# A fused attention and two-stage mixing kernel on one core: v of head 0, the staging of w_theta, the branch flag and the queue of loads are rearranged

## Chip, core and metric

The kernel runs on one core of one Trainium2 chip. The metric is the device time of one execution in microseconds (us); lower is better. The time before is the median of three runs, and one further execution was profiled.

## What is computed

Three layers follow each other, all in float32, for a batch of 2, 8 heads, 768 positions and 64 columns per head (so 16 heads in all and a model width of 512):

```python
# attention: a key counts if it is one of the first n_global or among the last n_local positions
scores = q @ k.T / sqrt(64) + bias                       # bias: -slope(head) * distance
a = softmax(where(keep, scores, -1e9)); x = a @ v        # heads side by side: x is 768 x 512
# mixing layer
theta = x @ w_theta
y = w_tok_r @ (x * cos(theta)) + w_tok_i @ (x * sin(theta))
u = x + y;  x2 = u + relu(u @ w_ch)
# feed-forward layer with a gate
h = relu(x2 @ w_in);  out = (h * sigmoid(conv3(h))) @ w_out
```

n_global is 8 and n_local is 96 here. The weights arrive as float64 bit patterns and are turned into float32 on the chip.

## The kernel before, in words

**Head of the program.** `begin` (line 1031) loads the two integers, q and k of heads 0 and 1, and builds the bias table. The integers decide by a flag (`fi`, line 1072) which of two programs runs: the fast one when both are small enough, a general one otherwise. Every engine loads the flag into a register (line 1022) and branches (line 1025). On VectorE that load stands behind the five instructions that finish the bias table (lines 1076 to 1080). Behind the branch, `run_fast` (line 860) makes ScalarE and GpSimd clear halves of staging tiles (lines 865, 866), lets GpSimd scale the bias table for head 1 (`tables`, line 336), and starts SyncE's queue with v of head 0 (`load_v`, line 274), q and k of heads 2 and 3 (`pair`) and v of head 1.

**Attention as a pipeline of steps.** The loop at line 903 counts steps j. Step j = 3i + tp treats head i, two blocks of 128 queries at a time. In step j TensorE makes the scores of step j; VectorE the bias, minimum and copy of step j-1 (`softmax`, line 372); ScalarE the exponentials of j-2 (line 381); TensorE the transposes of j-3 (line 390); ScalarE copies those of j-4 out (line 84); TensorE multiplies with v for j-5; and VectorE divides a finished head by its row sums (`normalise`, lines 290 to 292). Each engine works through its own list in the order in which the Python program emits it, and waits on semaphores only. So a "step" orders the list of an engine; it does not hold a queue back until TensorE gets there.

**Two ways of preparing q and k.** Heads 0 to 7 (`WHOLE`) are used as float32 straight from the load. Heads 8 to 15 are split into a rounded high part and a low part. For head i+1 this is done during head i: ScalarE makes the high part of q (line 300, at tp 0), VectorE its low part (line 304, at tp 1), and VectorE the low part of k (line 92, at tp 2). The high part of k is not computed: GpSimd's queue loads k a second time with a cast (`keys`, line 256, "the casting load", 408 KB), at tp 2, into the buffer that the head before the last one has just finished with. The low part of k needs this casting load and a plain load of k.

**SyncE's queue.** For heads 8 to 15 the plain loads are q (384 KB) at tp 2 of head i-3, k's second copy (204 KB) at tp 0 of head i-2 (both line 251), and v (357.5 KB) at tp 0 of the head itself. SyncE issues them strictly in the order of its list, each as soon as the buffer's last reader is done.

**The weight conveyor.** `Net.weight` queues a job per weight block, `Net.fetch` (line 121) puts its load on SyncE's queue when its staging tile is free, and `Net.conveyor` spends a few instructions on it per step: one on ScalarE (line 100), three on VectorE (lines 104, 108, 112), then the rounding (line 84) and the rest (line 92). Through the attention stage there are two staging tiles, `wst0` and `wst1`, which the jobs use in turn: jobs 0 to 3 are w_theta, jobs 4 to 11 the first half of w_tok. The next job but one is fetched when the third VectorE instruction of a job has freed its tile. The conveyor rests while heads 8 to 10 run (line 967).

Of the kernel before, what the change touches and what calls it, by code (L numbers as in the profile page):

```python
# [12 lines left out]
F32 = mybir.dt.float32  # L13
F32R = mybir.dt.float32r
I32 = mybir.dt.int32
# [4 lines left out]
B, H, S, D = 2, 8, 768, 64  # L20
DM, DFF = H * D, 1024
P = 128
# [3 lines left out]
NH = B * H  # L26
# [6 lines left out]
NV = 2 * NT - 1  # L33
VW = D + 1
HALF = S // 2
SLOT = 3072
STAGE = S + NT * KW
# [5 lines left out]
WHOLE = range(8)  # L43
# [9 lines left out]
class Net:  # L53
# [67 lines left out]
    def fetch(self):  # L121

        while self.loaded < self.limit:
            j = self.jobs[self.loaded]
            tag, x = j["where"]
            w = 2 * j["width"]
            if tag not in self.open or any(t == tag and x < b and a < x + w for t, a, b in self.held.values()):
                return
            self.held[self.loaded] = (tag, x, x + w)
            if tag == "scratch":  # L130
                j["st"] = self.head["scratch"][:, x : x + w].bitcast(I32)
            else:
                j["st"] = self.small.tile([P, 1024], I32, tag=tag, name=self.uid(tag))[:, :w]
            self.nc.sync.dma_start(j["st"], j["src"].bitcast(I32))
            self.loaded += 1
# [91 lines left out]
class Attention:  # L227
# [48 lines left out]
    def V(self, i):  # L276
        return self.v[i % 3].rearrange("p (t c) -> p t c", t=NV)
# [29 lines left out]
class FastAttention(Attention):  # L307
# [3 lines left out]
    def __init__(self, net, xs):  # L311
# [4 lines left out]
        self.whole = [x[:, 0:S], x[:, STAGE : STAGE + S], y[:, STAGE : STAGE + S], y[:, 0:S]]  # L316
        self.both = [x[:, S:STAGE], y[:, S:STAGE]]

    def half(self, i):
        return slice(D * (i % 2), D * (i % 2) + D)  # L320

# [138 lines left out]
class Mix:  # L460
# [6 lines left out]
    def begin(self):  # L467
        n = self.net
        self.xT = [n.slot(f"xT{b}", [P, KC, S], F32, "xT") for b in range(2)]
        wth = n.slot("w", [P, 2, KC, DM], F32R, "wth")  # L470
        self.wth = [wth[:, i] for i in range(2)]
        self.r = n.slot("r", [P, NT, DM], F32, "r")
        src = n.io["w_theta"].rearrange("(c p) n -> c p n", p=P)
        for c in range(KC):
            n.weight(src[c], DM, lambda c=c: (self.wth[0][:, c], self.wth[1][:, c]), (f"wst{c % 2}", 0))
        self.wt = [[n.slot("p0", [P, 4, 2, HALF], F32R, "wt"), n.slot("p1", [P, 4, 2, HALF], F32R, "wt"), None], [None] * 3]
        self.wch, self.win, self.wout = [None] * KC, [None] * NF, [None] * NF
        ring = [("wst0", 0), ("wst1", 0), ("scratch", 0), ("scratch", 2 * HALF), ("scratch", 4 * HALF)]
        for x in range(2 * NT * 2):
            hf, k = divmod(x, 2 * NT)  # L480
            s, ri = divmod(k, 2)

            def tok(hf=hf, k=k):
                w = self.wt[hf][k // 4]
                return None if w is None else (w[:, k % 4, 0], w[:, k % 4, 1])

            n.weight(n.io["w_tok"][NT * ri + s, :, HALF * hf : HALF * hf + HALF], HALF, tok, ring[k % 5] if hf else ring[k % 2])

        def of(ws, i):
            return lambda: None if ws[i] is None else (ws[i][:, 0], ws[i][:, 1])  # L490

        ring = [("wst0", 0), ("wst1", 0), ("scratch", 0)]
        src = n.io["w_ch"].rearrange("(c p) n -> c p n", p=P)
        late = [(src[c], self.wch, c) for c in range(KC)]
        late += [(n.io["w_in"][f], self.win, f) for f in (6, 7, 0, 1, 2, 3, 4, 5)]
        src = n.io["w_out"].rearrange("(f p) n -> f p n", p=P)
        late += [(src[f], self.wout, f) for f in range(NF)]
        for x, (src, ws, i) in enumerate(late):
            n.weight(src, DM, of(ws, i), ring[x % 3] if x < KC + NF else ring[x % 2])
        n.open = {"wst0", "wst1"}  # L500
        n.limit = 12

    def alloc_xTs(self):
# [194 lines left out]
    def tail(self, early):  # L698
# [20 lines left out]
            self.theta_part(t, th[t], (3,))  # L719
        ring.extend((("O", 2), ("O", 2), ("X", 1), ("PT", 2)))  # L720
        banks = [bank() for _ in range(KC)]
        turns = n.small.tile([P, 1024], I32, tag="wst0", name=n.uid("turns")).bitcast(F32)
        red = [self.reduce_theta(th[t], r[t], turns[:, DM * t : DM * t + DM]) for t in range(2)]
        for chain in (red[0], red[1], early, red[0]):
            next(chain, None)
# [134 lines left out]
def run_fast(tc, net):  # L860
# [2 lines left out]
    att = FastAttention(net, xs)  # L863
    mix = Mix(net, xs)
    nc.scalar.activation(att.whole[3][0:D], net.head["half_pi"][0:D].to_broadcast([D, S]), AF.Copy, scale=0.0)
    nc.gpsimd.memset(att.whole[2][D:P], 0.0)
    att.tables(1)
    att.load_v(0)
    att.pair(2)
    att.load_v(1)  # L870
    mix.begin()
# [31 lines left out]
    for j in range(NJ + LAG_N + 3):  # L903
# [14 lines left out]
        if 0 <= j - LAG_PV < NJ:  # L918
            att.pv(j - LAG_PV)
        jj = j - LAG_N  # L920
        for h in range(NH):
            if jj == 3 * h + 2 + (h in LATER):
                att.normalise(h, att.o.pop(h))
# [5 lines left out]
        if i > 0 and i + 1 not in WHOLE:  # L929
            if tp == 0:  # L930
                att.split(i + 1, "  A")
            else:
                att.split(i + 1, ("   V", " V")[tp - 1])
        if tp == 1 and i > 0 and i + 2 in WHOLE and i % 2 == 0:
            att.pair(i + 2)
        if tp == 2 and i + 3 < NH and i + 3 not in WHOLE:
            att.load(i + 3, slice(0, S))
        if tp == 0 and i + 2 < NH and i + 2 not in WHOLE:
            att.load(i + 2, slice(S, STAGE), slice(D, P))
        if i > 0 and tp == 2 and i + 1 in WHOLE:  # L940
            att.load_v(i + 1)
        if tp == 0 and i < NH and i not in WHOLE:
            att.load_v(i)
        last.step()
        jj = j - LAG_N - 1
# [18 lines left out]
            next(early, None)  # L964
        if j == 4:
            net.fetch()
        if 6 < j < NJ and i not in (8, 9, 10):
            net.run((3, 2, 3)[tp] if i > 10 else 2)
    last.drain()
# [3 lines left out]
def run_general(tc, net):  # L973
# [5 lines left out]
    for i in range(NH):  # L979
# [5 lines left out]
            att.unit(i, t, o)  # L985
        att.normalise(i, o)
    mix.begin()
    net.finish(12)
    for b in range(2):
        mix.alloc_xTs()  # L990
# [25 lines left out]
def build(nc, io):  # L1016
    with tile.TileContext(nc) as tc, tc.tile_pool(name="const", bufs=1) as small:
        head = {}
        net = Net(tc, io, small, None, None, head)
        with tc.tile_pool(name="idle", bufs=1, space=bass.MemoryType.PSUM) as ps, tc.manual_schedule():  # L1020
            begin(nc, io, net, small, head, ps.tile([P, 512], F32, name="idle"))
        rv = nc.values_load(
            head["flag"][:1, :1], min_val=0, max_val=1, skip_runtime_bounds_check_because="it is the product of comparisons, 0 or 1"
        )
        with tc.If(rv == 1) as cmp:
            arm(tc, io, head, run_fast)
        with cmp.Else():
            arm(tc, io, head, run_general)
# [2 lines left out]
def begin(nc, io, net, small, head, idle):  # L1031
# [4 lines left out]
    for x in range(0, NT, 2):  # L1036
        k, q = slice(x * KW, x * KW + 2 * KW), slice(x * P, x * P + 2 * P)
        nc.scalar.dma_start(scratch[:, S:STAGE][:, k], io["pairs"][0, :, k])
        nc.sync.dma_start(scratch[0:D, q], io["qk"][0, 0:D, 0, q])
    nc.sync.dma_start(scratch[D:P, STAGE : STAGE + S], io["qk"][0, D:P, 1, 0:S])  # L1040
    nc.vector.memset(scratch[D:P, 0:S], 0.0)
    zero = nc.const_aps.tensor(0.0, [P, 512], F32)
    for x in (512, 512, 256):
# [29 lines left out]
    far = small.tile([P, NG], F32, name="far")  # L1073
    nc.gpsimd.tensor_scalar(far, R[:, G], ng, BIG, op0=ALU.is_ge, op1=ALU.mult)
    nc.gpsimd.tensor_scalar(far, far, nl, FIRST, op0=ALU.max, op1=ALU.mult)
    nc.vector.tensor_scalar(T, R, 1.0 / FIRST, nl, op0=ALU.mult, op1=ALU.is_ge)  # L1076
    nc.vector.scalar_tensor_tensor(T, T, FIRST * BIG, R, op0=ALU.mult, op1=ALU.min)  # L1077
    nc.vector.tensor_copy(X, T[:, O])
    nc.vector.tensor_tensor(X[:, 0:NG], X[:, 0:NG], far, op=ALU.max)
    nc.vector.tensor_copy(T[:, G], far)  # L1080
    nnl = small.tile([P, 1], F32, name="nnl")
    head.update(scratch=scratch, qk0=qk0, table=table, ident=ident, half_pi=hp[:, 0:1], ng=ng, nl=nl, nnl=nnl, flag=fi)


# [34 lines left out]
```

## Time and profile before

| | us |
|---|---|
| median of three runs | 405.25 (404.54, 405.25, 405.83) |
| the profiled execution, its own time | 404.36 |
| span of that execution, first to last instruction | 402.6 |

The span is cut into instructions per engine. TensorE appears twice: PE is its matmuls, PEld its weight loads. DVE is VectorE, ACT ScalarE, POOL GpSimd, SP SyncE. A group's row gives how often it ran, its busy time and mean duration, and how long the engine idled before it and on whom it waited. The chain of waits is followed from the last instruction backwards, at each step to whatever released it. The timeline gives start and duration of each instruction or run of like instructions. DMA rows say how long a load took from issue to landing.

### The profile page before, as it was taken

To read this page: it belongs to the slowest core of one execution; us is meant where nothing else is said; L and a number is where in the kernel's file an instruction comes from. 1 tells how busy PE (TensorE), PEld (TensorE's weight loads), DVE (VectorE), ACT (ScalarE), POOL (GpSimd) and SP (SyncE) were. 2 spreads that over 40 slices of the span, in tenths; PEclk is the share of its full clock that TensorE was granted. 3 is DMA by queue.
4 is the path that set the end of the run, shared out by engine and by line. 5 is a ranking of instruction groups with operands and counts; after the bars stand their busy time and mean duration, and the time that the engine had idled before them with its cause. 6 is when DMAs were issued, how large, how long until landed. Compare 5 with 4: busy or idle time off the path is not lost.

```text
span 402.6 us, 6479 instructions
## 1 busy us (share of the span) xinstructions
PE 396.0 (98%) x2382; PEld 374.4 (93%) x2382; DVE 321.8 (80%) x708; ACT 224.7 (56%) x439; POOL 26.0 (6%) x36
## 2 busy tenths in 40 slices
PE   8999999999999999999999999999999999999995
PEld 5999999999988999999999999999999998888885
DVE  6788999998878869999899999998999999700001
ACT  5888888787887787235355346555654554300000
POOL 5214123121000000000000000000000000000000
PEclk9999999999999999999999999999999999999998
DMA  7978798855000330246464433130000000210111
GB/s 191 314 230 247 216 268 232 246 153 157 0 2 0 117 89 33 78 145 172 155 206 163 157 104 106 53 105 2 0 2 0 2 0 2 78 52 34 45 52 60
DMA packets 16023, 42.94 MB, mean 107 GB/s; under 512 B 2160, under 2 KB 2992, under 8 KB 15984
## 3 DMA queue, kind: packets, MB, share of 16 engines
q1 hardware_dynamic: 13968, 38.44, 30.8%
q0 software_dynamic: 1152, 3.34, 3.0%
q10 hardware_dynamic: 864, 0.68, 0.6%
q8 instruction: 20, 0.33, 0.3%
q14 instruction: 19, 0.16, 0.1%
HBM read 39.31 MB, written 3.15 MB: 105 GB/s over the span
## 4 chain that ended last, share of the span: by engine, by line
PE 96%; DMA 2%; DVE 1%; issue 0%; DVEq 0%
PE O L95 26%; PE S L95 23%; PE PT L95 17%; PE TH L95 15%; PE X L95 9%; PE PT L390 4%; DMA qk<-qk 1%; PE X L514 1%; DMA words<-n 1%; DVE qk L92 0%; DVE scratch L88 0%; DVE table L1077 0%; PE TH L514 0%; PE O L514 0%; DVE table L1076 0%
## 5 line engine op out<-in xcount | busy, mean ns | idle before, releaser
L381 ACT ACTIVATE a<-a,nm 128x232 f32<-128x232 f32 (+1 forms) x96 | 39.8, 466 | 4.7 <-DVE nm L372 4.6
L95 PE MATMUL O<-a,a 128*128 128x65 f32 x236 | 29.9, 268 | 0.0
L100 ACT ACTIVATE wbit<-wst 128x512 f32<-128x512 f32 (+1 forms) x38 | 23.2, 614 | 11.2 <-DMA wst<-w_ch 4.7
L95 PEld LDWEIGHTS O<-a,a 128*128 128x128 f32 x236 | 29.0, 192 | 0.2
L84 ACT ACTIVATE a<-PT 128x512 f32<-128x512 f32 (+1 forms) x48 | 26.5, 552 | 3.8 <-PE PT L390 3.6
L372 DVE CUSTOM_DVE_ANT_0 a<-S,qk 128x232 f32<-128x232 f32 (+1 forms) x72 | 24.0, 371 | 5.0 <-PE PT L390 4.9
L390 PE MATMUL PT<-ident,a 128*128 128x128 f32 x176 | 27.1, 273 | 0.0
L95 PE MATMUL O<-wt,z 128*128 128x384 f32 x144 | 26.9, 334 | 0.0
L95 PE MATMUL TH<-wth,xTs 128*128 128x512 f32 x96 | 26.2, 408 | 0.0
L104 DVE TENSOR_SCALAR wbit<-wbit 128x512 int32<-128x512 int32 (+1 forms) x48 | 18.9, 395 | 8.7 <-ACT wbit L100 8.7
L95 PE MATMUL PT<-wt,z 128*128 128x384 f32 x132 | 25.8, 334 | 0.0
L84 ACT ACTIVATE wt<-wbit 128x384 fp32r<-128x384 f32 x24 | 12.5, 520 | 23.3 <-DVE wbit L112 13.7
L95 PEld LDWEIGHTS O<-wt,z 128*128 128x128 f32 x144 | 25.2, 188 | 0.1
L112 DVE SCALAR_TENSOR_TENSOR wbit<-wst,wbit 128x512 int32<-128x512 int32 (+1 forms) x38 | 23.8, 627 | 1.1
L108 DVE SCALAR_TENSOR_TENSOR wbit<-wst,wbit 128x512 int32<-128x512 int32 (+1 forms) x38 | 23.8, 626 | 1.0
L95 PEld LDWEIGHTS PT<-wt,z 128*128 128x128 f32 x132 | 23.1, 188 | 0.0
L390 PEld LDWEIGHTS PT<-ident,a 128*128 128x128 f32 x176 | 20.8, 141 | 1.3
L95 PE MATMUL S<-wt,z 128*128 128x384 f32 x120 | 22.0, 335 | 0.0
L336 POOL TENSOR_SCALAR qk<-table 128x360 fp32r<-128x360 f32 x15 | 18.3, 1222 | 41.2 <-DVE nm L372 28.8
L95 PEld LDWEIGHTS S<-wt,z 128*128 128x128 f32 x120 | 20.9, 188 | 0.0
L95 PEld LDWEIGHTS TH<-wth,xTs 128*128 128x128 f32 x96 | 17.0, 189 | 3.1
L95 PE MATMUL O<-x,win 128*128 128x384 f32 x96 | 17.4, 336 | 0.0
(216 smaller groups left out, 940.6 us busy)
## 6 DMA issues: line engine op xcount, KB each, us to landing
wst<-w_tok SPq DMA_DIRECT2D x18, 384.0 KB, 3.5
a<-v SPq DMA_DIRECT2D x16, 357.5 KB, 5.2
wst<-w_out SPq DMA_DIRECT2D x8, 512.0 KB, 3.2
qk<-qk POOLq DMA_DIRECT2D x8, 408.0 KB, 5.4
a<-qk SPq DMA_DIRECT2D x8, 384.0 KB, 5.0
out<-scratch SPq DMA_DIRECT2D x11, 256.0 KB, 2.0
wst<-w_in SPq DMA_DIRECT2D x5, 512.0 KB, 4.3
scratch<-w_tok SPq DMA_DIRECT2D x6, 384.0 KB, 3.4
```

The lines of the kernel that those rows point to most:

```text
L84: self.nc.scalar.activation(out, in_, AF.Copy)
L95: self.nc.tensor.matmul(out, l, r, start=start, stop=stop)
L100: self.nc.scalar.activation(t.bitcast(F32), w[:, 1 : w.shape[1] : 2].bitcast(F32), AF.Copy, scale=REBIAS)
L104: self.nc.vector.tensor_scalar(t, t, 3, None, op0=ALU.logical_shift_left)
L108: self.nc.vector.scalar_tensor_tensor(t, w[:, 0 : w.shape[1] : 2], 29, t, op0=ALU.logical_shift_right, op1=ALU.bitwise_or)
L112: self.nc.vector.scalar_tensor_tensor(t, w[:, 1 : w.shape[1] : 2], -(1 << 31), t, op0=ALU.bitwise_and, op1=ALU.bitwise_or)
L336: self.nc.gpsimd.tensor_scalar(self.bias[i % 2], self.net.head["table"], x / FIRST, None, op0=ALU.mult)
L372: self.nc.vector.tensor_tensor_reduce(self.sS[tp][:, c], s["sp"][:, c], t, scale=QSCALE if i in WHOLE else 1.0, scalar=3.0e38, op0=ALU.add ...
L381: self.nc.scalar.activation(sS[:, c], sS[:, c], AF.Exp, bias=s["nm"][:, u : u + 1], scale=-1.0)
L390: self.nc.tensor.transpose(pt[:, c], sS[:, self.columns(u, a)], net.head["ident"])
L514: self.nc.tensor.transpose(xb[:, P * jj : P * jj + P], self.xs[b][:, t, P * c : P * c + P], n.head["ident"])
```

## The change

Seven edits go together:

1. v of head 0 gets a place in `wst0`, which becomes a tile of `begin`, and is loaded there ahead of the branch, behind the loads of q and k. `load_v(0)` goes from `run_fast`.
2. `wst0` is thus closed to the conveyor until step 9. The four w_theta jobs are staged in `wst1` and in the tile `r`, which nothing uses until theta is reduced. Later jobs use `wst0` and `wst1` as before.
3. Every engine's flag load is emitted ahead of VectorE's five bias-table instructions, where only VectorE's own order changes.
4. GpSimd scales the table of head 1 before it clears its half tile, not after.
5. At tp 2, VectorE's low part of k comes before `normalise`, not after.
6. The plain loads of q move from tp 2 of head i-3 to tp 0 of head i-2, those of k's second copy from tp 0 to tp 1, and those of v from tp 0 to tp 1. The casting load keeps tp 2 and is the only one emitted there.
7. The general program opens `wst0` before it drains the conveyor, and the tail names `wst0` directly.

```diff
     def fetch(self):
...
-            if tag == "scratch":
-                j["st"] = self.head["scratch"][:, x : x + w].bitcast(I32)
+            if tag in self.head:
+                j["st"] = self.head[tag][:, x : x + w].bitcast(I32)
...
+    def V(self, i):
+        return super().V(i) if i else self.net.head["v0"].rearrange("p (t c) -> p t c", t=NV)
...
-            n.weight(src[c], DM, lambda c=c: (self.wth[0][:, c], self.wth[1][:, c]), (f"wst{c % 2}", 0))
+            n.weight(src[c], DM, lambda c=c: (self.wth[0][:, c], self.wth[1][:, c]), (("wst1", "r")[c % 2], 0))
...
-        n.open = {"wst0", "wst1"}
+        n.open = {"wst1", "r"}
...
     nc.scalar.activation(att.whole[3][0:D], net.head["half_pi"][0:D].to_broadcast([D, S]), AF.Copy, scale=0.0)
+    att.tables(1)
     nc.gpsimd.memset(att.whole[2][D:P], 0.0)
-    att.tables(1)
-    att.load_v(0)
     att.pair(2)
...
         jj = j - LAG_N
+        if tp == 2 and i > 0 and i + 1 not in WHOLE:
+            att.split(i + 1, " V")
         for h in range(NH):
             if jj == 3 * h + 2 + (h in LATER):
                 att.normalise(h, att.o.pop(h))
...
             if tp == 0:
                 att.split(i + 1, "  A")
-            else:
-                att.split(i + 1, ("   V", " V")[tp - 1])
+            elif tp == 1:
+                att.split(i + 1, "   V")
...
-        if tp == 2 and i + 3 < NH and i + 3 not in WHOLE:
-            att.load(i + 3, slice(0, S))
-        if tp == 0 and i + 2 < NH and i + 2 not in WHOLE:
-            att.load(i + 2, slice(S, STAGE), slice(D, P))
+        if tp < 2 and i + 2 < NH and i + 2 not in WHOLE:
+            att.load(i + 2, *((slice(0, S),), (slice(S, STAGE), slice(D, P)))[tp])
         if i > 0 and tp == 2 and i + 1 in WHOLE:
             att.load_v(i + 1)
-        if tp == 0 and i < NH and i not in WHOLE:
+        if tp == 1 and i < NH and i not in WHOLE:
             att.load_v(i)
...
+        if j == LAG_PV + 4:
+            net.open.add("wst0")
...
-        rv = nc.values_load(
-            head["flag"][:1, :1], min_val=0, max_val=1, skip_runtime_bounds_check_because="it is the product of comparisons, 0 or 1"
-        )
-        with tc.If(rv == 1) as cmp:
+        with tc.If(head["fits"] == 1) as cmp:
...
     nc.sync.dma_start(scratch[D:P, STAGE : STAGE + S], io["qk"][0, D:P, 1, 0:S])
+    wst0 = small.tile([P, 1024], F32, name="wst0")
+    v0 = wst0[:, 0 : NV * VW]
+    nc.sync.dma_start(v0, io["v"][0, 0])
...
     nc.gpsimd.tensor_scalar(far, far, nl, FIRST, op0=ALU.max, op1=ALU.mult)
+    fits = nc.values_load(fi[:1, :1], min_val=0, max_val=1, skip_runtime_bounds_check_because="it is the product of comparisons, 0 or 1")
     nc.vector.tensor_scalar(T, R, 1.0 / FIRST, nl, op0=ALU.mult, op1=ALU.is_ge)
```

## Rows read from the trace of the kernel before

**Rows 1.** Windows: us, busy (instructions) of PE, PEld, DVE, ACT, POOL; clock, DMA share, GB/s.
```profile
0.00:5.30 5.30, 4.01 (x7) 1.74 (x7) 3.12 (x11) 1.84 (x3) 2.45 (x13) 1.00 0.52 132
...
34.00:57.50 23.50, 23.47 (x195) 22.78 (x193) 22.96 (x79) 20.74 (x48) 6.43 (x6) 1.00 0.82 239
...
58.80:86.90 28.10, 27.38 (x209) 25.60 (x209) 27.00 (x80) 23.23 (x51) 6.77 (x8) 1.00 0.83 240
```

**Rows 2.** The waits, whole span: waiting engine and line, releaser, us, times, longest.
```profile
PEld S L95 <- DVE qk L92: 1.0, 2, 0.9
```

**Rows 3.** The chain of waits at head 10: start us, us, what.
```profile
52.92 5.76 DMA qk<-qk
...
59.77 0.71 PE S L95 x4
```

**Rows 4.** Timeline, steps 29 and 30: start us, us, instruction [idle before <-releaser].
```profile
57.53 0.17 DVE L290 TENSOR_SCALAR rs<-O 128x6 f32<-128x6 f32 x1
...
57.96 0.56 DVE L292 TENSOR_TENSOR xs<-O,rs 128x384 f32<-128x384 f32 x1
...
58.71 1.00 DVE L92 TENSOR_TENSOR qk<-a,qk 64x816 fp32r<-64x816 f32 x1 [0.20 <-DMA qk<-qk]
...
59.77 0.52 PEld L95 LDWEIGHTS S<-qk 128*128 128x128 f32 x4 [0.86 <-DVE qk L92]
```

**Rows 5.** Timeline, the start of the program.
```profile
5.06 0.73 POOL L866 MEMSET xs<- 64x768 f32 x1 [0.32 <-DVE table L1077]
5.26 1.30 PEld L95 LDWEIGHTS S<-scratch 128*128 128x128 f32 x8 [0.89 <-issue]
...
6.88 0.69 PEld L95 LDWEIGHTS TH<-scratch 128*128 128x128 f32 x4 [0.32 <-issue]
...
6.92 0.29 DVE L372 CUSTOM_DVE_ANT_0 a<-S,table 128x128 f32<-128x128 f32 x1 [0.69 <-PE S L95]
...
8.39 0.49 PE L390 MATMUL PT<-ident,a 128*128 128x128 f32 x3
```

**Rows 6.** Line 1022, the flag load, by engine: duration ns min/median/max, start us.
```profile
L1022 PEldq TENSOR_LOAD <-fi x1: 491/491/491, 4.3 to 4.3; - x1
L1022 DVEq TENSOR_LOAD <-fi x1: 542/542/542, 6.1 to 6.1; - x1
```

**Rows 7.** Line 1038, the three loads of k of heads 0 and 1.
```profile
DMA to landing us min/median/max: 3.0/3.3/4.7
```

**Rows 8.** SyncE's issues, 42 to 53 us: start us, us, load (x2: two in a row).
```profile
42.07 3.01 SPq L251 DMA_DIRECT2D a<-qk  x2
48.79 0.33 SPq L134 DMA_DIRECT2D wst<-w_tok  x1
...
52.14 2.14 SPq L251 DMA_DIRECT2D a<-qk  x2
```

**Rows 9.** Line 251, plain loads of q and k, 30 to 52 us.
```profile
DMA to landing us min/median/max: 4.9/5.8/6.7
```

**Rows 10.** Timeline: preparing q of head 10; low parts and first scores of heads 11, 12.
```profile
53.84 0.84 ACT L300 ACTIVATE qk<-a 128x768 fp32r<-128x768 f32 x1
...
55.88 0.95 DVE L304 SCALAR_TENSOR_TENSOR qk<-a,qk 128x768 fp32r<-128x768 f32 x1
...
63.88 1.00 DVE L92 TENSOR_TENSOR qk<-a,qk 64x816 fp32r<-64x816 f32 x1
...
65.35 0.69 PE L95 MATMUL S<-qk 128*128 128x128 f32 x4
...
71.60 1.00 DVE L92 TENSOR_TENSOR qk<-a,qk 64x816 fp32r<-64x816 f32 x1
...
73.23 0.61 PE L95 MATMUL S<-qk 128*128 128x128 f32 x4
```

**Rows 11.** Line 256, the eight casting loads, whole span.
```profile
DMA to landing us min/median/max: 4.1/5.4/8.0
```

**Rows 12.** The DMA view, 50 to 59 us: packets and rate.
```profile
DMA packets 888, 2.39 MB, mean 266 GB/s; under 512 B 110, under 2 KB 110, under 8 KB 887
```

More of the change, by code (lines that the diff above doesn't have):

```diff
@@ L472, in begin @@
         self.r = n.slot("r", [P, NT, DM], F32, "r")
+        n.head["r"] = self.r.rearrange("p t d -> p (t d)")
         src = n.io["w_theta"].rearrange("(c p) n -> c p n", p=P)
         for c in range(KC):
-            n.weight(src[c], DM, lambda c=c: (self.wth[0][:, c], self.wth[1][:, c]), (f"wst{c % 2}", 0))
+            n.weight(src[c], DM, lambda c=c: (self.wth[0][:, c], self.wth[1][:, c]), (("wst1", "r")[c % 2], 0))
         self.wt = [[n.slot("p0", [P, 4, 2, HALF], F32R, "wt"), n.slot("p1", [P, 4, 2, HALF], F32R, "wt"), None], [None] * 3]
@@ L721, in tail @@
         banks = [bank() for _ in range(KC)]
-        turns = n.small.tile([P, 1024], I32, tag="wst0", name=n.uid("turns")).bitcast(F32)
+        turns = n.head["wst0"]
         red = [self.reduce_theta(th[t], r[t], turns[:, DM * t : DM * t + DM]) for t in range(2)]
@@ L987, in run_general @@
     mix.begin()
+    net.open.add("wst0")
     net.finish(12)
@@ L1081, in begin @@
     nnl = small.tile([P, 1], F32, name="nnl")
-    head.update(scratch=scratch, qk0=qk0, table=table, ident=ident, half_pi=hp[:, 0:1], ng=ng, nl=nl, nnl=nnl, flag=fi)
+    head.update(scratch=scratch, wst0=wst0, v0=v0, qk0=qk0, table=table, ident=ident, half_pi=hp[:, 0:1], ng=ng, nl=nl, nnl=nnl, fits=fits)
 def kernel(q, k, v, n_global, n_local, moe_w_theta, moe_w_tok_r, moe_w_tok_i, moe_w_ch, moe2_w_in, moe2_conv_w, moe2_w_out):
```

## The prediction

> **What bounds the kernel now.** I read the busy times by stretch first. TensorE is the engine to watch: from 34.0 to 57.5 us it is busy 23.47 of 23.50 us, and the granted clock is 1.00 in each stretch shown, its 2.4 GHz level [rows 1]. So time can be won only where TensorE stands still, and the change touches no matmul. Up to 5.3 us it does no useful work [rows 1]. After that, the list of waits names one culprit: its weight loads waited 1.0 us in all, in two places, for VectorE's line 92, the low part of k, and one of the two was 0.9 us [rows 2]. The chain shows where: the casting load of head 10 is issued at 52.92 us, lands 5.76 us later, the low part runs, and head 10's first scores start at 59.77 [rows 3]. TensorE had been ready 0.86 us earlier [rows 4]. That is nearly all there is to win.
>
> The second thing to see is VectorE. It is busy 22.96 of 23.50 us before this place and 27.00 of 28.10 us after it [rows 1]. TensorE has work for about the same time, so VectorE trails it with no reserve: what VectorE loses here, TensorE meets again as a late operand.
>
> **Start: v of head 0, flag, table.** VectorE now loads its flag before the table is finished. A load takes 0.54 us there [rows 6]. If it holds up the five instructions behind it, the table is late by as much; in return the 0.69 us before VectorE's first softmax, which the load and branch fill today, shrink [rows 5]. TensorE's own flag load waits for the same flag as before and takes 0.49 us from 4.3 us [rows 6], so its first scores stay at 5.26 us [rows 5]. The first transposes at 8.39 follow the scores without a wait [rows 5]. So this edit costs nothing on the path; its cover is TensorE's 3 us of scores, and without that it would be worth between minus and plus 0.54 us. Clearing GpSimd's half tile (0.73 us [rows 5]) after the table of head 1 costs nothing either: step 6 is the first to read the tile, and without that cover it costs the 0.73 us.
>
> v's load now leaves SyncE's queue about 1.5 us sooner, behind q and k, and the loads behind it on that queue follow one issue earlier. It reaches the DMA engines while the third load of k may still run. TensorE stood 0.32 us before the third pair of scores, which need that load [rows 5]. The three equal loads took 3.0, 3.3 and 4.7 us [rows 7]. Bounds: the whole 0.32 us won, or 1.7 us lost if v does to the third load what crowding did between the fastest and the slowest. I take +0.1: v stands last in its queue, far nearer to no effect.
>
> **Weights in r, and what that does to SyncE's queue.** r is not written until theta is reduced, so staging there waits for nothing. With three tiles for jobs 0 to 5, jobs 4 and 5 are fetched one place sooner; jobs 6 and 7 keep theirs, because they wait for the tiles of jobs 4 and 5.
>
> SyncE issues in list order, so moving a load by a step matters only if something is overtaken. I went through the list. Around heads 9 to 11 it was: job 6, k(9), q(10), job 7, k(10), v(8), q(11), k(11), v(9). It becomes: job 6, q(9), k(9), job 7, q(10), k(10), v(8), q(11), k(11), v(9). **q(11) does not move**: it was issued at 52.14 us, when the low part of q(9) freed its buffer, and that still frees it then. So the casting load at 52.92 us is "alone" in the emission, not on the DMA engines. **q(10) does move**: it was the second of the two loads at 42.07 to 45.08 us, and now stands behind job 7, which waits until 48.79 us [rows 8]. So 384 KB, 1.48 us at the 266 GB/s of 50 to 59 us [rows 12], come into the stretch in which the casting load runs.
>
> q(10) is needed at 53.84 by ScalarE and, through it, at 55.88 by VectorE [rows 10]. Issued at 49.1 and landing within 4.9 to 6.7 us [rows 9], it arrives between 54.0 and 55.8. ScalarE then waits 0.2 to 2.0 us, and queued behind it are the next exponentials and copies, which TensorE needs two steps later. VectorE is held up only beyond 55.0 (55.88 less 0.84), by 0.8 us at most, and then waits for the casting load anyway. I take 0; bounds 0 and 0.8.
>
> **Low part of k ahead of normalise.** Step 29 is the only step in which a normalise and a low part of k fall together. Today VectorE normalises head 7 from 57.53 to 58.52 us (0.99 us), then idles 0.20 us for the casting load, then makes the low part in 1.00 us [rows 4]. Afterwards it waits first, and normalise, a cast and the next softmax queue behind that wait. All hangs on L, when the casting load of head 10 lands:
>
> - L up to 57.53: the low part ends at 58.53, TensorE starts when it is ready, 0.86 us sooner. Normalise ends at 59.52, VectorE is 0.19 us ahead of its 59.71. The low part for head 11 then ends at 64.69 instead of 64.88, and scores follow one in 0.06 us (59.71 to 59.77), so head 11 starts at 64.75 instead of 65.35 [rows 4, 10]. Of the 0.86 us, 0.60 survive.
> - L as today, 58.68: head 10 starts at 59.77 as before, but VectorE is 0.99 us late. Head 11's low part ends at 65.87, its scores start at 65.93: **0.58 us lost**. Head 12's low part would end at 73.59 and its scores could start at 73.65, before 73.81, when TensorE gets there [rows 10]; nothing more is lost.
> - In between, and beyond, each 0.1 us of L is 0.1 us of time. The edit breaks even at 58.10, 5.18 us after the issue.
>
> The eight casting loads took 4.1 to 8.0 us, median 5.4 [rows 11]. I take today's 5.76 us: the neighbours that crowded it are still there, and q(10) is added, partly into time in which the DMA engines were less than full (0.82 [rows 1]).
>
> The Trainium skill says otherwise. Its page "DMA: Bandwidth & Descriptors", section "Anatomy of one DMA — SWDGE (gpsimd) path", fits about 2.0 us plus bytes over 436 GB/s for a load issued by GpSimd; for 418 kB that is an estimate of 2.96 us, L would be 55.9, and the sum would be the first case. The rows never show under 4.1.
>
> **Sum.** +0.58 for the order on VectorE, +0.1 for the start, 0 for the rest: +0.68. The profiled execution, 404.36 us (span 402.6 and 1.76 around it), would become 405.04. It lay 0.89 under the median of the runs, 405.25; on that, 405.9.
>
> **Rivals.**
>
> 1. *The casting load does get through.* It lands by about 57.5, 4.6 us after its issue. For it: half of its kind took 5.4 us or less, one 4.1 [rows 11]. Against it: nothing that was on the DMA engines beside it goes away. Gain 0.60, with no loss at the start: 404.65. Chance 0.25 (all landings that win anything).
> 2. *Slower: q(10)'s bytes delay the casting load.* Place: 50 to 58 us, SyncE's loads and the casting load on the same engines. If all 1.48 us go into L, it is 60.16, head 11 starts 2.06 us late, with the start 2.16: 407.4. It decides (over 0.3% slower) from L = 59.2, 6.3 us after the issue. For it: casting loads of up to 8.0 us [rows 11]. Against: it needs nearly half of those bytes in L. Chance 0.22.
> The same page, under "Issuing engines are not separate DMA queues", says that loads from all engines run on the same 16 and interleave, whoever issues them; by that rule, too, order on SyncE's queue does not give the casting load room.
> 3. *The change does not do what it says*: the queue delivers at the same times, and VectorE idles little. That is L near 58.1 and 0 to 0.1 us: 405.3. Chance 0.13.
>
> **How the numbers follow.** My forecast has 0.40; its own range, from the start's bounds and L within 0.4 us, is 405.2 to 406.6. The range over all cases goes from 404.3 (first rival, and the 0.32 us at the start) to 407.0, which leaves out the end of the second rival and the far bound of the start, together well under 2 in 10. A measurement of this kernel tells about 0.3%, 1.2 us, from no change. Faster by more needs 404.03, beyond even the 0.60 and 0.32 us together unless the medians scatter (the three runs spread over 1.3 us): 0.12. Slower by more is the second rival and the upper edge of the forecast: 0.24. The rest, 0.64, is within.
>
> **What would show it.** In the profile after: first scores still near 5.26. q(10)'s issue near 49 us. VectorE's low part of k ahead of lines 290 to 292 at step 29, with idle time of about 1.2 us before it on the casting load. TensorE's wait at head 10 about as long as now, and a new one of about half a microsecond on line 92 at head 11. The prediction is wrong if the casting load of head 10 lands within 5 us, if head 10's wait is gone with none at head 11, or if TensorE waits for ScalarE's exponentials near 57 us.

## The result, and the profile after

The kernel after takes **408.87 us** (median; 407.43 to 410.60 over six runs) against 404.95 (404.54 to 405.83, six runs) for the kernel before: ratio 1.0098, 95% interval 1.0074 to 1.0122. It is slower, and above the upper end of the forecast range (407.0). The profiled execution took 407.71 us, its span is 405.9 instead of 402.6.

The 3.3 us of the span lie in three places: about 0.5 at the start, 1.3 in a longer standstill of TensorE at head 10, and the rest, some 1.6, in a stretch after it in which TensorE ran at half its clock. (The end of the program gave 0.1 back.)

The chain of waits of the kernel after at head 10 (start us, us, what), beside [rows 3]:

```profile
53.44 7.07 DMA qk<-qk
...
60.53 1.02 DVE qk L92
...
61.59 0.71 PE S L95 x4
```

The casting load of head 10 takes 7.07 us instead of 5.76. The timeline shows who waits for it and in which order, beside [rows 4, 10]:

```profile
55.48 0.85 ACT L300 ACTIVATE qk<-a 128x768 fp32r<-128x768 f32 x1 [1.02 <-DMA a<-qk]
...
60.53 1.00 DVE L92 TENSOR_TENSOR qk<-a,qk 64x816 fp32r<-64x816 f32 x1 [2.55 <-DMA qk<-qk]
...
61.57 0.17 DVE L290 TENSOR_SCALAR rs<-O 128x6 f32<-128x6 f32 x1
61.59 0.52 PEld L95 LDWEIGHTS S<-qk 128*128 128x128 f32 x4 [2.17 <-DVE qk L92]
```

VectorE idles 2.55 us, makes the low part of k, and only then normalises; TensorE stands still for 2.17 us where it stood for 0.86. SyncE's issues (start us, us, load), beside [rows 8], show the cause that the forecast had named: the second line is q and k of head 10, behind job 7.

```profile
49.30 0.33 SPq L134 DMA_DIRECT2D wst<-w_tok  x1
49.72 1.97 SPq L251 DMA_DIRECT2D a<-qk  x2
...
52.66 2.15 SPq L251 DMA_DIRECT2D a<-qk  x2
```

q of head 10 landed 5.7 us after its issue, near 55.46. What that does to the casting load is seen by queue. The DMA view from 53.5 to 56.5 us (q1 is SyncE's queue, q0 GpSimd's; packets, MB, share of 16 engines), first of the kernel before, then of the kernel after:

```profile
q1 hardware_dynamic: 229, 0.60, 66.7%
q0 software_dynamic: 119, 0.37, 36.6%
```

```profile
q1 hardware_dynamic: 372, 0.97, 100.5%
q0 software_dynamic: 10, 0.03, 3.0%
```

In these three microseconds the casting load, issued 0.5 us later than before, moved 10 packets instead of 119: SyncE's loads filled the engines alone. The engines had been full there in the kernel before too (66.7% and 36.6%); what changed is whose packets filled them.

The windows of the kernel after (columns as in [rows 1]) show what no part of the forecast had:

```profile
60.00:61.60 1.60, 0.01 (x1) 0.01 (x1) 1.04 (x2) 0.96 (x2) 0.00 (x0) 1.00 1.07 343
61.60:63.00 1.40, 1.40 (x13) 1.40 (x13) 1.33 (x5) 0.00 (x0) 0.00 (x0) 1.00 0.52 140
63.00:66.50 3.50, 3.50 (x20) 3.50 (x19) 3.50 (x15) 2.69 (x7) 1.67 (x1) 0.52 0.51 161
66.50:68.00 1.50, 1.50 (x16) 1.50 (x16) 1.06 (x3) 0.68 (x3) 0.00 (x0) 0.99 0.72 162
```

TensorE stands still up to 61.6, works again, and from 63.0 to 66.5 us its granted clock is 0.52, so nearly all of that stretch is at the 1.2 GHz level. At full clock the same matmuls would have taken 1.82 us (3.50 by 0.52), so up to 1.7 us go there. In the kernel before, the clock is 1.00 through all of this. The first scores of head 11, beside [rows 10]:

```profile
68.79 0.69 PE L95 MATMUL S<-qk 128*128 128x128 f32 x4
```

TensorE was not idle in between. It restarts at head 10 1.82 us later than in the kernel before (61.59 against 59.77) and reaches head 11 3.44 us later (68.79 against 65.35), so 1.62 us are the clock's alone. From there to its last matmul it stays 3.4 to 3.5 us late.

At the start (beside [rows 5, 7]) the first scores hardly moved, the third pair did:

```profile
5.37 1.30 PEld L95 LDWEIGHTS S<-scratch 128*128 128x128 f32 x8 [0.71 <-issue]
...
7.40 0.69 PEld L95 LDWEIGHTS TH<-scratch 128*128 128x128 f32 x4 [0.72 <-issue]
```

### The profile page after: what moved, and what is told of

Same layout as the page of the kernel before. It is cut to its first block, busy times and chain, and to the rows that moved or that the text cites. A ratio compares the mean times of both kernels' runs of the same rounds, so it can differ in the third digit from the quotient of the medians.

```text
span 405.9 us, 6466 instructions
## 1 busy us (share of the span) xinstructions
PE 398.2 (98%) x2382; PEld 376.2 (93%) x2382; DVE 321.5 (79%) x708; ACT 225.3 (56%) x439; POOL 25.9 (6%) x36
## 4 chain that ended last, share of the span: by engine, by line
PE 95%; DMA 3%; DVE 0%; ACTq 0%; issue 0%; DVEq 0%
PE O L95 26%; PE S L95 23%; PE PT L95 16%; PE TH L95 15%; PE X L95 9%; PE PT L393 4%; DMA qk<-qk 2%; DMA scratch<-pairs 1%; PE X L518 1%; DVE qk L92 0%; ACTq L1041 0%; DVE scratch L88 0%; ACTq L1038 0%; PE TH L518 0%; PE O L518 0%
## 5 line engine op out<-in xcount | busy, mean ns | idle before, releaser
L95 PE MATMUL O<-a,a 128*128 128x65 f32 x220 | 28.1, 269 | 0.0
L100 ACT ACTIVATE wbit<-wst 128x512 f32<-128x512 f32 (+1 forms) x36 | 21.8, 609 | 10.4 <-DMA wst<-w_ch 2.7
L95 PEld LDWEIGHTS O<-a,a 128*128 128x128 f32 x220 | 27.2, 193 | 0.2
L112 DVE SCALAR_TENSOR_TENSOR wbit<-wst,wbit 128x512 int32<-128x512 int32 (+1 forms) x36 | 22.5, 624 | 1.1
L108 DVE SCALAR_TENSOR_TENSOR wbit<-wst,wbit 128x512 int32<-128x512 int32 (+1 forms) x36 | 22.5, 624 | 0.9
```

What stands on the lines that cost most here:

```text
L95: self.nc.tensor.matmul(out, l, r, start=start, stop=stop)
L100: self.nc.scalar.activation(t.bitcast(F32), w[:, 1 : w.shape[1] : 2].bitcast(F32), AF.Copy, scale=REBIAS)
L108: self.nc.vector.scalar_tensor_tensor(t, w[:, 0 : w.shape[1] : 2], 29, t, op0=ALU.logical_shift_right, op1=ALU.bitwise_or)
L112: self.nc.vector.scalar_tensor_tensor(t, w[:, 1 : w.shape[1] : 2], -(1 << 31), t, op0=ALU.bitwise_and, op1=ALU.bitwise_or)
```

## The experiments

Time before is the median measured beside each group of runs; times are medians, "ratio" is to the kernel before.

| run | what | us | before | ratio, 95% interval |
|---|---|---|---|---|
| e1_loads_back | after, edit 6 undone | 405.13 | 404.55 | 0.9992 to 1.0021 |
| e2_loads_moved | before, edit 6 alone | 408.51 | 404.55 | 1.0051 to 1.0105 |
| e3_v0_behind | after, v of head 0 behind the branch | 408.67 | 404.55 | 1.0057 to 1.0120 |
| e4_keep_busy | after, ten matmuls in the standstill, waiting ones | 412.78 | 404.55 | 1.0167 to 1.0230 |
| e5_keep_busy2 | after, ten matmuls in the standstill | 407.37 | 404.67 | 1.0043 to 1.0076 |
| e6_job7_late | after, job 7 at step 31 | 405.45 | 404.67 | 1.0013 to 1.0032 |
| e7_before_job7 | before, job 7 at step 31 | 404.77 | 404.67 | 0.9998 to 1.0016 |
| e8_before_job7_k_first | e7 with edit 5 | 405.26 | 404.67 | 1.0005 to 1.0022 |
| e9_q_back | after, only q's loads put back | 405.46 | 404.91 | 1.0007 to 1.0027 |
| e10_start_only | after, edits 5 and 6 undone | 405.06 | 404.91 | 0.9995 to 1.0013 |
| e11_split | before, edit 5, casting load of head 10 in two | 405.07 | 404.91 | 0.9998 to 1.0017 |
| e12_split_job7 | e11 with job 7 at step 31 | 405.14 | 404.91 | 0.9994 to 1.0032 |
| e13_followers_late | e8, job 7 at 34, k of 11 and v of 9 later | 410.60 | 404.64 | 1.0116 to 1.0158 |
| e14_split_later | e12 with job 7 at step 34 | 405.87 | 404.64 | 1.0025 to 1.0074 |
| e15_split2_later | e14, head 11's casting load in two as well | 405.20 | 404.64 | 1.0006 to 1.0023 |
| e16_split2_32 | e15 with job 7 at step 32 | 404.26 | 404.77 | 0.9975 to 0.9993 |
| e17_split_32 | e14 with job 7 at step 32 | 405.05 | 404.77 | 1.0000 to 1.0020 |

**Which edit costs it.** e1 takes edit 6 out of the kernel after, e2 puts it alone into the kernel before:

```diff
-        if tp < 2 and i + 2 < NH and i + 2 not in WHOLE:
-            att.load(i + 2, *((slice(0, S),), (slice(S, STAGE), slice(D, P)))[tp])
+        if tp == 2 and i + 3 < NH and i + 3 not in WHOLE:
+            att.load(i + 3, slice(0, S))
+        if tp == 0 and i + 2 < NH and i + 2 not in WHOLE:
+            att.load(i + 2, slice(S, STAGE), slice(D, P))
...
-        if tp == 1 and i < NH and i not in WHOLE:
+        if tp == 0 and i < NH and i not in WHOLE:
             att.load_v(i)
```

> The kernel after, with the moves of the plain loads (edit 6) undone and the other six edits kept. Theory A (the order of loads puts q of head 10 beside the casting load of head 10): q of head 10 leaves SyncE's queue near 45 us instead of 49.7, the casting load of head 10 takes 6 us or less instead of 7.07, TensorE's wait for the low part of k at head 10 is 0.9 us or less instead of 2.2, the granted clock stays at 1.00 from 60 to 68 us, and the time is 405.3 to 406.3 us: the 0.5 us of the start stay, and up to 0.6 us for the low part ahead of normalise. Rival B (the casting load is late because of the weights staged in r, or by chance): the casting load still takes about 7 us, the wait is still about 2 us, and the time stays within 1 us of 408.9.

> The kernel before, with the moves of the plain loads (edit 6) alone. Theory A: q of head 10 leaves near 49 us, the casting load of head 10 takes 6.5 to 7.5 us, TensorE waits 1.9 to 3.0 us at head 10 (normalise comes first here, but is done before the load lands), the granted clock falls to about 0.5 for some us after it, and the time is 407.2 to 408.5 us. Rival B: casting load 5.8 us as in the kernel before, wait 0.9 us, no fall of the clock, 405 us.

Both as theory A said: without edit 6 the loss is gone (the time, 405.13, even just below the forecast), and edit 6 alone brings 3.96 us (408.51 less 404.55; by the interval of the ratio, 2.1 to 4.2). Rival B falls. The casting load took 5.2 us in e1 and 8.0 in e2, where TensorE stood still for 3.1 us, both a little above what theory A gave. And the clock fell for longer than in the kernel after (windows of e2):

```profile
60.00:62.00 2.00, 0.00 (x0) 0.00 (x0) 0.64 (x1) 1.09 (x2) 0.00 (x0) 1.00 1.03 345
62.00:64.00 2.00, 1.58 (x7) 1.58 (x8) 1.97 (x7) 0.69 (x2) 0.24 (x1) 0.54 0.59 151
64.00:66.00 2.00, 2.00 (x12) 2.00 (x11) 1.86 (x6) 0.66 (x2) 1.43 (x1) 0.50 0.79 255
66.00:68.00 2.00, 2.00 (x12) 2.00 (x11) 0.20 (x1) 1.16 (x3) 0.00 (x0) 0.50 0.53 114
68.00:70.00 2.00, 2.00 (x16) 2.00 (x15) 1.62 (x5) 0.75 (x2) 0.00 (x0) 0.75 0.24 91
```

**Which load of edit 6.** e9 leaves k and v where the change put them and puts back q alone (the first condition of the diff above), so that q of head 10 passes ahead of job 7 again.

> The kernel after, with only the loads of q put back to tp 2 of head i-3; k's second copy and v stay at tp 1. The list of SyncE then has q of head 10 ahead of job 7. Theory A (q of head 10 alone is what crowds the casting load): q of head 10 leaves by 46 us, the casting load of head 10 takes 5.2 to 6.2 us as in every kernel so far with that load early, TensorE's wait at head 10 is at most 1 us, the clock stays at 1.00, and the time is 405.0 to 405.8 us. Rival H (k and v moved by a step matter as well): the casting load takes 6.5 us or more, 406.5 us or more.

The chain of waits of e9 at head 10:

```profile
53.05 5.70 DMA qk<-qk
58.76 1.02 DVE qk L92
59.82 0.71 PE S L95 x4
```

That is the kernel before again [rows 3]; rival H falls. One load, 384 KB issued at 49.7 instead of 44.8 us, carries most of the loss: 3.4 of the 3.9 us (408.87 less 405.46). The 0.55 us that e9 still loses (405.46 less 404.91) are close to the +0.68 that the prediction worked out for a casting load of 5.76 us; here it took 5.70.

**The start.** e3 issues v of head 0 first behind the branch; e10 has the edits of the start and the staging in r alone.

```diff
-    nc.sync.dma_start(v0, io["v"][0, 0])
...
+    nc.sync.dma_start(net.head["v0"], io["v"][0, 0])
     att.pair(2)
```

> The kernel after, with the load of v of head 0 issued first behind the branch, as in the kernel before, but still into wst0. Theory C (v of head 0, sent before the branch, crowds the third load of k): the third load takes about 4.7 us instead of 5.2, the third pair of scores starts 0.4 to 0.5 us sooner, the span shrinks by 0.4 to 0.5 us if the rest repeats. Rival D (the flag loaded early, or the order of the table, made TensorE's start late): the third pair of scores stays at 7.4 us, time unchanged. Head 10 is as in the kernel after by both.

> The kernel after, with the moves of the loads and the low part of k ahead of normalise (edits 5 and 6) undone: what is left is v of head 0, the staging in r, the flag and the table. Theory: the third load of k takes about 0.3 us longer than in the kernel before and TensorE starts as much later; head 10 is as in the kernel before (wait 0.6 to 0.9 us), with no new wait at head 11: 404.7 to 405.3 us. Rival: staging in r or the flag costs something of its own, over 405.5 us.

e3's third load of k took 4.97 us instead of 5.19 and its third pair of scores started at 7.18 us, 0.22 sooner: the direction of theory C, half its size, and the time (408.67 against 408.87) can't be told from the same. In e10 the third load took 5.46 us, and yet the time is within the interval of no change, so the staging in r and the flag cost nothing that can be seen. Over all the traces, the load took 4.75 to 5.62 us (mean 5.12) in the seven with v ahead of the branch and 4.67 to 5.01 (mean 4.84) in the twelve with v behind it: 0.3 us for the start, with ranges that overlap.

**The clock.** e4 and e5 put ten matmuls ahead of head 10's first scores, into the tile that those overwrite. In e4 they read k of head 9, whose buffer the casting load of head 11 was already filling, so they waited for it; e5 reads q of head 9 twice instead.

```diff
+        if j == 30:
+            H9 = self.Q(9)[:, 0]
+            for x in range(10):
+                net.mm(sp[:, 0:RW], H9[:, 0:P], H9[:, 0:RW], True, True)
```

> The kernel after, with ten extra matmuls (128x232, one pass each) on operands of head 9 put ahead of the first scores of head 10, into the same tile that those scores then overwrite; they add work, and the output is the same. Theory E (the granted clock falls because TensorE stood still for over 2 us): the ten matmuls take about 1.7 us of the 2.2 us of standing still, the casting load still lands near 60.5 us, the granted clock stays at 1.00 from 60 to 68 us, and the time falls by 1.2 to 2.5 us to 406.4 to 407.7. Rival F (the fall of the clock has another cause, or costs nothing because VectorE sets the pace): clock 0.5 again near 63 us or no gain, time within 0.5 us of 408.9.

> The kernel after, with ten extra matmuls (128x232, one pass) ahead of the first scores of head 10, into the tile that those scores then overwrite; both operands are now the high part of q of head 9, which no load touches then, so that they wait for nothing. They add work; the output is the same. Theory E (the granted clock falls because TensorE stood still for over 2 us): the ten take about 1.3 us of the standing still, starting near 59.4 us, the casting load still lands between 60 and 61.5 us, what is left of the wait is about 1 us as in the kernel before, the granted clock stays at 1.00 from 60 to 70 us, and the time falls to 406.0 to 407.3 us. Rival F (the fall of the clock has another cause, or costs nothing because VectorE sets the pace after the stall): clock 0.5 again near 63 us or no gain, time within 0.5 us of 408.7.

e4 missed what it was for, and became the longer standstill: 4.5 us, after which the windows have the clock at 0.50 until 72 us:

```profile
62.00:64.00 2.00, 0.44 (x2) 0.47 (x3) 1.96 (x8) 0.00 (x0) 0.00 (x0) 0.50 0.47 138
...
70.00:72.00 2.00, 2.00 (x12) 2.00 (x11) 0.91 (x5) 1.41 (x4) 0.00 (x0) 0.50 0.53 172
```

In e5 the casting load landed as late as ever (7.8 us, at 61.3), and 1.65 us of standstill were left, but the clock stayed up:

```profile
60.00:62.00 2.00, 0.96 (x9) 0.77 (x7) 0.64 (x1) 1.70 (x3) 0.00 (x0) 1.00 1.03 362
62.00:64.00 2.00, 1.58 (x14) 1.58 (x15) 1.90 (x6) 0.00 (x0) 0.00 (x0) 1.00 0.64 176
64.00:66.00 2.00, 2.00 (x21) 2.00 (x20) 2.00 (x10) 1.81 (x5) 1.35 (x1) 1.00 0.81 263
```

More work, and 1.5 us less time (407.37 against 408.87), just above theory E's range; rival F falls. In the traces, e5 restarts at head 10 0.83 us later than the kernel after (62.42 against 61.59), and its last matmul still starts 0.31 us sooner (400.93 against 401.24).

The size of the clock's share is seen best within one program. These are the executions of the three kernels in which q of head 10 stands behind job 7 and TensorE has no extra work (the kernel after, e2, e3), by the mean granted clock of the execution:

| mean granted clock | executions | us |
|---|---|---|
| 0.997 to 1.000 | 4 | 406.00 to 407.43 |
| 0.996 | 3 | 407.70 to 409.03 |
| 0.993, 0.994 | 7 | 407.71 to 408.81 |
| 0.990 | 7 | 409.77 to 410.60 |

Where a trace was kept, 0.993 and 0.994 had one stretch of 3.4 us at the lower level at head 10, and 0.990 had 6.8 us of it. The medians (406.5 at the top, 408.4 at 0.993 and 0.994, 410.1 at the bottom) lie about 1.8 us apart. Executions in which the clock stayed up are still about 2 us above the kernel before: what is left is the longer standstill and the start.

**What sets the casting load's time.** e6 to e8 hold job 7 back:

```diff
+    net.limit = 7
...
+        if j == 31:
+            net.limit = 12
+            net.fetch()
```

> The kernel after, with weight job 7 (393 KB, not needed before head 11) held back until step 31, so that it stands neither in front of q of head 10 nor beside the casting load. Theory A: q of head 10 leaves SyncE's queue by 46 us, the casting load of head 10, with some 780 KB less around it, takes 5 us or less, TensorE's wait at head 10 is under 0.5 us, the clock stays at 1.00, and the time is 404.3 to 405.3 us (start 0.5 us late still in it). Rival G (the bytes do not matter, the casting load is slow beside any other load): it takes 5.8 us or more and the time is 405.5 us or more.

> The kernel before, with job 7 held back in the same way. Theory A: the casting load of head 10, with 393 KB less ahead of it, takes 4.5 to 5.2 us instead of 5.8, lands by 58.2 us; VectorE normalises first until 58.5 us, so TensorE's wait at head 10 falls from 0.86 to about 0.7 us and the time to 404.2 to 404.8 us. Rival G: nothing changes, 404.6 us or more.

> The kernel before, with job 7 held back and the low part of k ahead of normalise (edit 5). Theory A: the casting load lands by 58.0 us, the low part follows at once, TensorE's wait at head 10 is under 0.5 us, and the time is 403.7 to 404.4 us, below both kernels. Rival G: the casting load still takes 5.8 us, the low part is no sooner and normalise is late: 404.8 us or more.

e6 removes most of the loss, as theory A said, but misses its bounds for the load (5.55 us), the wait (0.65) and the time (405.45), and in e7 and e8 rival G is right: the casting load took 5.6, 6.2 and 5.8 us in the three, against 5.8 in the kernel before. Job 7's own bytes were not beside it: in the kernel after they landed 3.4 us after 49.30, before the casting load was issued. e13 turns to the other side, the loads issued behind it (k of head 11, v of head 9):

```diff
-        if tp == 0 and i + 2 < NH and i + 2 not in WHOLE:
+        if tp == 0 and i != 9 and i + 2 < NH and i + 2 not in WHOLE:
...
+        if j == 29:
+            att.load(11, slice(S, STAGE), slice(D, P))
+            att.load_v(9)
```

> The kernel before, with the low part of k ahead of normalise, job 7 held back until step 34, and k's second copy of head 11 and v of head 9 put behind q of head 12 in SyncE's list (they then leave after 57 us instead of 53.8 and 54.4). Theory K (the loads issued behind the casting load of head 10 stretch its tail): nothing runs beside it but q of head 11, and it takes 4.5 us or less, landing by 57.6 us; TensorE's wait at head 10 is below 0.2 us; the crowd moves to the casting load of head 11, issued at 58.3, which takes over 5.5 us. Rival L (the loads ahead of it, or its own cost, set its time): it still takes 5.2 us or more. No forecast of the time beyond the wait at head 11: 404 to 406 us.

The casting load of head 10 in e13:

```profile
DMA to landing us min/median/max: 4.3/4.3/4.3
```

Theory K holds: 1.6 us less than e8's 5.8, no wait at head 10. So it is slowed by both: by what is still queued at its issue (the kernel after, e2) and by what follows it (e13). The forecast of the whole failed: head 11's casting load took 7.3 us in the crowd, TensorE waited 0.5 us for v and 1.7 us for k, and the clock fell in all four runs.

**Can the standstill be won?** e11, e12, and e14 to e17 cut casting loads in two, so that the first columns leave one step sooner. Below, "the same" of e17 means e16, whose text stands last:

```diff
-            self.nc.gpsimd.dma_start(self.K(i), self.net.io["qk"][b, :, h, S:STAGE])
+            self.nc.gpsimd.dma_start(self.K(i)[:, c], self.net.io["qk"][b, :, h, S:STAGE][:, c])
...
+        if tp == 1 and i == 8:
+            att.keys(10, slice(0, 3 * KW + SKIP))
```

> The kernel before, with the low part of k ahead of normalise, and the casting load of head 10 cut in two pieces: columns 0 to 439 issued after the scores of step 25, the rest after step 26. Theory I (the casting load is late because its bytes start to move only after its buffer is free, 52.9 us, and then queue behind q of head 11): the first piece lands by 57.5 us, the second, with less than half of the bytes, by 58.0 us, TensorE's wait at head 10 falls below 0.3 us, head 11 waits under 0.2 us, and the time is 403.7 to 404.4 us. Rival J (what takes the time is the last packets and the landing itself, whatever the size): the second piece lands at 58.5 us or later, 404.8 us or more.

> The same, with job 7 held back until step 31 too. Theory I: the first piece finds the queues nearly empty and lands by 56 us, the second by 57.8 us, no wait over 0.2 us at head 10 or 11, 403.6 to 404.3 us. Rival J: as above, 404.8 us or more.

> The kernel before, low part of k ahead of normalise, the casting load of head 10 in two pieces, job 7 held back until step 34 (it then leaves after 62 us). Theory: no wait at head 10 as in the run with job 7 at step 31; the casting load of head 11, without job 7 beside it, takes 5 us or less instead of 6.5, so TensorE's wait at head 11 falls from 1.4 to under 0.4 us; 403.7 to 404.5 us against 404.9 for the kernel before. Rival: k of head 12 and v of head 10 beside it are enough, the wait at head 11 stays at 1 us or more, 404.8 us or more.

> The same, with the casting load of head 11 cut in two pieces as well. Theory: no wait over 0.2 us at head 10 or 11, 403.5 to 404.2 us. Rival: as above.

> The same with only head 10's casting load cut. Theory: the wait at head 11 is 0.7 to 1.0 us, 404.2 to 404.8 us. Rival: as above, 404.8 us or more.

> The kernel before, low part of k ahead of normalise, the casting loads of heads 10 and 11 in two pieces each, job 7 held back until step 32 (it then leaves near 63 us, behind q of head 13). Theory (the two new waits were job 7's place): no wait at head 10, under 0.8 us at head 11, none over 0.3 us on ScalarE near 75 us, 403.9 to 404.5 us against 404.6 to 404.9 for the kernel before. Rival (the wait moves to whatever is late next): the sum of TensorE's waits between 58 and 80 us stays at 0.9 us or more and the time at 404.7 us or more.

In e11 rival J won (the second piece landed at 59.1). In e12 the two pieces of head 10 were quick and the casting load of head 11 was not:

```profile
DMA to landing us min/median/max: 2.7/3.1/3.5
...
DMA to landing us min/median/max: 6.5/6.5/6.5
```

The wait had moved to head 11 (1.4 us), and in two of eleven runs (408.7 and 408.9 us) the clock fell there. With job 7 at step 34 (e14, e15) the wait at head 11 shrank to 0.9 and 0.7 us (in three of e14's twelve runs the clock fell all the same) and a new one of 1.2 us came up, because ScalarE, in e15, stood in front of job 7's data:

```profile
72.55 0.55 ACT L100 ACTIVATE wbit<-wst 128x384 f32<-128x384 f32 x1 [3.04 <-DMA wst<-w_tok]
```

e17 still waits 1.1 us at head 11. e12, e14, e15 and e17 all missed the times of their theories and ended where their rivals had put them, at 404.8 us or more. Only e16, with both casting loads cut and job 7 between (it left at 63.78 us), has none of these; all that its weight loads wait for by the list of waits, above 0.5 us:

```profile
PEld idle L95 <- issue: 2.6, 5, 0.7
PEld S L95 <- issue: 1.0, 1, 1.0
PEld TH L95 <- issue: 0.6, 1, 0.6
```

It is the one version below both kernels: 404.26 us, ratio 0.9984, a gain of 0.3 to 1.0 us by the interval. The theory's forecast held.

## Why the prediction was wrong

- **The step that failed** is "I take today's 5.76 us" for the casting load of head 10. It took 7.07, and 7.1 to 8.0 in the five traces in which q of head 10 stands behind job 7, against 5.2 to 6.2 in the seven with that q early and the load uncut and its followers in place. The reason given, that q's bytes go partly into time in which the engines were less than full, used a mean (0.82 over 23 us). At the place itself, 53.5 to 56.5 us, the engines were full in the kernel before, and in the kernel after SyncE's queue alone took 100.5%. By the prediction's own rule the 1.31 us more in L turn its +0.68 into +2.0. That is about what the executions with the clock up show (406.0 to 407.4 us, against 404.6 to 405.0 before).
- **A term left out** is the clock. The prediction had read 1.00 in every stretch shown and gave a fall no price. It costs 1.6 us in the trace of the kernel after, and about 1.8 us for each such stretch by the table of executions; the median, 408.87, lies between the executions with one and those with two of them.
- **Rival 2 had the mechanism** and the place, and got 0.22. It put all 1.48 us of q's bytes into the casting load, 7.24 us in place of the 7.07 found. Its price of 407.4 was short by the clock: the one execution of the kernel after with the clock at 1.00 took 407.43. It was also held against this rival that it "needs nearly half of those bytes"; by the sum, 1.2 us less the 0.68 already forecast, it needs 0.52 of 1.48, a third.
- **The forecast's own range**, 405.2 to 406.6, does not come out of the bounds it names: 0.32 us won to 1.7 lost at the start and 0.4 us either way in L give 405.1 to 407.9. The measured time lies above both.
- **The signs of being wrong** were badly chosen: none of the three came. What gave the miss away were the two forecasts beside them, VectorE's idle time (2.55 us, not 1.2) and TensorE's wait at head 10 (2.17 us, not 0.86).
- **q of head 10 on ScalarE**: landing forecast 54.0 to 55.8, found 55.46; ScalarE waited 1.02 us, and the low part of q at 56.40 still came before VectorE's wait for k. Taken as 0, and right.
- **Low part of k ahead of normalise**: right in mechanism, and in size wherever the clock stayed up. The forecast wait of "about half a microsecond" at head 11 is absent from the kernel after, where TensorE at half clock came late enough, but stands in e1 (0.47), e6, e8 and e9. TensorE's waits in e8, whose casting load took 5.82 us:

```profile
60.14 0.52 PEld L95 LDWEIGHTS S<-qk 128*128 128x128 f32 x4 [0.91 <-DVE qk L92]
66.19 0.52 PEld L95 LDWEIGHTS S<-qk 128*128 128x128 f32 x4 [0.41 <-DVE qk L92]
```

  With loads of 5.20, 5.55, 5.70 and 5.82 us (e1, e6, e9, e8) the traces lost 0.00, 0.31, 0.46 and 0.56 us against the kernel before between heads 9 and 12. The prediction's rule, even at 5.18 and 0.1 us for each 0.1 us beyond, gives 0.02, 0.37, 0.52 and 0.64.
- **The start**: the sign was right, the size not: 0.3 us over all traces, 0.5 in the profiled one, against +0.1. The first scores moved by 0.11 us, the flag cost nothing, as forecast.
- **Rival 1** did not come near: the whole load never took under 3.5 us in any trace, and that of head 10 never under 4.2. The estimate of 2.96 us came from the fit on the page "DMA: Bandwidth & Descriptors" of the Trainium skill, section "Anatomy of one DMA — SWDGE (gpsimd) path"; here only halves of the load came near it, on emptied queues (2.7 us in e12). That loads of all engines run on the same 16 and interleave, as the same page of the Trainium skill says under "Issuing engines are not separate DMA queues", the traces bear out in its first half: SyncE's loads are what the GpSimd load waits for. How they interleave varied: in the three microseconds shown above it was 119 packets to 229 in the kernel before, and 10 to 372 in the kernel after.

## What to carry to other kernels

When a load is moved in a queue, look up what its new neighbours are in the microseconds before the critical load is issued and just after it, by queue and not by a mean share: one 384 KB load behind a blocked entry of an in-order list was worth 3.4 us. Price a standstill of TensorE with the stretch behind it, since the clock may fall there. And expect a wait that is removed to turn up at the next consumer of the same resource: here it took the low part of k put first, two split loads and one weight load moved, all together, to win half a microsecond (404.77 to 404.26), where the list of waits had offered 0.86.

## What the runs showed of the hardware

- After TensorE had stood still for 2.2 us (the kernel after) the granted clock was at its lower level for about 3.4 us, with 3.1 us of it for about 6.8 in e2 and 3.4 in e3, with 4.5 us (e4) for about 10; in e2 and e4 it fell before TensorE was at work again. Length alone does not decide: 1.65 us in e5 and 1.28 in e7 left the clock at 1.00, 1.4 us in e12 did not. Over the six runs of the kernel after the mean granted clock was 0.990 to 1.00, so the same program had, by that mean, none, one or about two such stretches. Even the kernel before had one execution in the 127 measured beside the experiments with a mean of 0.993, and it took 407.50 us. What decides in a single execution is not shown.
- A GpSimd load's first data packet came 1.6 us after its issue on emptied queues (e7) and 2.8 us after it in the kernel after. For head 10 it was 1.5 to 2.0 us in the seven traces with q early and the load uncut and its followers in place, and 2.8 to 3.5 us in the five with q behind job 7. So here the load did not share the engines at once with what SyncE had queued.
- VectorE's flag load does hold up the instructions behind it (4.30 to 4.84 us; 0.68 us idle ahead of line 1083). The table was ready only 0.1 us later all the same (6.33 against 6.24 us), because the copy at line 1085 took 0.23 us where it took 0.87 in the kernel before, beside GpSimd's clearing of the half tile. The copy took 0.23 us in all eight traces with this order and 0.86 to 0.87 in the other eleven. ScalarE's clearing ran beside the slow copies as well, so that GpSimd's is the cause is likely, not shown.
